# Seven products of quarters for eight in the last block's gate and value matmuls

## The chip, the cores and the metric

The kernel runs on one core of a Trainium2 chip. The metric is the device time of one execution in microseconds. The core's engines are TensorE (PE in the profile, its weight loads PEld), VectorE (DVE), ScalarE (ACT), GpSimd (POOL) and SyncE (SP), whose queue issues all DMA transfers of this kernel.

## The reference

Attention with a threshold (scores that lie more than tau below the row's maximum are dropped), followed by two gated layers; the first one normalises its input. Sizes: 4 batches, 8 heads, 576 positions, head size 64; so 2304 tokens of width 512, and an inner width of 1536. All data are float32.

```python
scores = scale * np.matmul(q, k.transpose(0, 1, 3, 2))
thresh = np.max(scores, axis=-1, keepdims=True) - tau
scores = np.where(scores >= thresh, scores, -1000000000.0)
scores = scores - np.max(scores, axis=-1, keepdims=True)
attn = np.exp(scores)
attn = attn / (np.sum(attn, axis=-1, keepdims=True) + 1e-09)
x = np.matmul(attn, v)                       # then tokens x (heads * 64)
xn = x / np.sqrt(np.mean(x * x, axis=-1, keepdims=True) + 1e-06) * rms_g
g = xn @ w_gate
x = (g * (1.0 / (1.0 + np.exp(-g)))) * (xn @ w_val) @ w_out
# second layer: the same with moe2_w_gate, moe2_w_val, moe2_w_out, without the norm
```

## The kernel before

The 2304 tokens are three blocks of 768 (`NB`, `TW`). A block's tokens lie along the columns: `X` holds its 4 chunks of 128 channels by 768 tokens. Attention of block 0 comes first and alone (`fast`); attention of block 1 and of block 2 (`tile_ops`, `pv`) is spread among the dense matmuls of the block before or two blocks before, so that the last block's dense matmuls run with no attention beside them.

The dense part (`moe`) has two layers of 18 units. Twelve units are gate-and-value units (`gate_val`), each for 128 of the 1536 inner channels; behind the fifth, the ninth and the twelfth of them come two units each of output products (`outp`). Every float32 operand is kept as a high and a low part in float32r, and a product is made of three matmuls (high by high, high by low, low by high). `dense` therefore issues, for one 128x768 result over 4 chunks of channels, 4 x 3 x 2 = 24 matmuls of 128x384, six to a piece; a gate-and-value unit has 48 of them. The results go by turns to two PSUM tiles of two banks each, `PB` and `PD` (`dense_ps`; in the profile all are `ps`, in the order of instructions ps1 and ps2). The gate's result goes through a tanh on ScalarE (L809) and a VectorE step (L810), the value's result through a second VectorE step (L821); `h`, the product, is split into its two parts by ScalarE (L825) and by VectorE or GpSimd (L828).

The weights of a unit are 128x1024 numbers. In block 0 they come from the inputs as 64-bit numbers and are converted (`weights`: three ScalarE steps, L737 to L739, and one on VectorE, L740), split into high and low part (`w_split`: ScalarE L702, VectorE or GpSimd L704) and stored to memory (`kept`). For the units in `K_E` only the whole number is stored and split again in blocks 1 and 2, for the others both parts are stored and loaded.

The order is made by a program at build time: each step has an engine, a cost in ns and a priority (`p=`), and a list scheduler (`Program.order`) goes through them, always taking on each engine the ready step with the smallest priority. The tables `NORM_E`, `HI_E`, `LO_E`, `V_E`, `W_E`, `H_E`, `X_E`, `P_E`, `EV_E` and `XO_E` choose the engine of steps that can run on more than one, and `UP`, `FP`, `T0`, `OFF`, `OFFF` and the like are the offsets of the priorities. Each engine then runs its queue strictly in that order.

Of the kernel before, what the change touches and what calls it, by code (L numbers as in the profile page):

```python
# [25 lines left out]
P = 128  # L26
# [9 lines left out]
NU = 18  # L36
# [47 lines left out]
NORM_E = [(0, 2, 0, 0, 2, 0, 0, 0, 1, 1, 0, 1), (1, 1, 1, 1, 0, 2, 1, 1, 2, 1, 1, 1), (1, 2, 2, 1, 0, 1, 1, 1, 0, 1, 2, 2)]  # L84
HI_E = [(2, 2, 2, 2, 2, 0, 1, 1, 1, 2, 2, 1), (2, 1, 0, 1, 0, 1, 0, 0, 1, 2, 2, 0), (0, 0, 0, 0, 0, 0, 1, 2, 2, 2, 0, 1)]
LO_E = [(0, 0, 2, 0, 2, 0, 0, 2, 2, 0, 0, 0), (0, 0, 2, 0, 2, 2, 0, 0, 0, 0, 0, 0), (0, 0, 2, 0, 2, 0, 0, 2, 0, 2, 0, 2)]


V_E = {0, 1, 4, 7, 8, 14, 15, 18, 20, 22, 25, 26, 27, 28, 29, 33, 35, 38, 41, 42, 44, 46, 47, 48, 50, 52, 57, 61}
# [12 lines left out]
EV_E = {0, 2, 5, 9, 12, 15, 20, 23, 27, 32, 33, 34, 37, 40, 43, 45, 46, 49, 51}
XO_E = {0, 2, 3, 4, 6, 8, 12, 17}
# [133 lines left out]
def body(ctx: ExitStack, tc: tile.TileContext, qkv, tau, w1, rg, w2, outT):  # L237
# [47 lines left out]
    r_raw = ring("raw", RAWN, [P, 2 * S], F32)  # L285
    r_v = ring("v", 3, [P, 5, 2, D], F32)
    r_v3 = ring("v3", 3, [P, 5, 64], BF16)
    ET = sb.tile([P, 4, S], F32, name="e")
# [22 lines left out]
    def SU(u):  # L311

        full = 36 * (NB - 1)
        if u <= full:
            return T0 + u * UP
        return T0 + full * UP + (u - full) * UL
# [649 lines left out]
```

## Time and profile before

| | |
|---|---|
| median of 3 runs | 1209.44 us (1208.04 to 1210.07) |
| profiled execution | 1210.33 us, of which the span of instructions 1208.5 us |
| mean granted TensorE clock | 0.997 |
| busy share of TensorE | 98% |
| busy shares of VectorE, ScalarE, GpSimd | 61%, 51%, 39% |
| last block behind its norm | from 898.8 to 1204.4 us of the span |

The profile gives each engine's busy time, tables of busy time by stretches, groups of instructions by line with their mean duration and the idle time before them, a list of who waited for whom, the chain of work that ended last, and the instructions in order of time. An end of a matmul is modelled, and matmuls overlap in the records: one lasts 0.34 us in them, while they start every 0.17 us.

### The profile page before, as it was taken

To read this page: it belongs to the slowest core of one execution; us is meant where nothing else is said; L and a number is where in the kernel's file an instruction comes from. 1 tells how busy PE (TensorE), PEld (TensorE's weight loads), DVE (VectorE), ACT (ScalarE), POOL (GpSimd) and SP (SyncE) were. 2 spreads that over 40 slices of the span, in tenths; PEclk is the share of its full clock that TensorE was granted. 3 is DMA by queue.
4 is the path that set the end of the run, shared out by engine and by line. 5 is a ranking of instruction groups with operands and counts; after the bars stand their busy time and mean duration, and the time that the engine had idled before them with its cause. 6 is when DMAs were issued, how large, how long until landed. Compare 5 with 4: busy or idle time off the path is not lost.

```text
span 1208.5 us, 18818 instructions
## 1 busy us (share of the span) xinstructions
PE 1178.9 (98%) x7252; PEld 1046.0 (87%) x7252; DVE 736.3 (61%) x1363; ACT 610.6 (51%) x827; POOL 468.2 (39%) x543
## 2 busy tenths in 40 slices
PE   7998889999999999999999999999999999999998
PEld 4565778888888888988888889888899999999998
DVE  7998686778868687576566576656543133332342
ACT  5779877878787877234434435434421222232211
POOL 1123256545666576434534636445320202220311
PEclk9999999999999999999999999999999999999999
DMA  7223758889689977665664554543344322212211
GB/s 231 87 87 130 277 147 267 264 224 266 185 232 244 252 236 191 149 198 155 177 146 112 125 146 110 124 128 75 92 135 145 105 88 70 93 65 87 71 53 53
DMA packets 173417, 181.98 MB, mean 151 GB/s; under 512 B 143760, under 2 KB 147344, under 8 KB 163344
## 3 DMA queue, kind: packets, MB, share of 16 engines
q1 hardware_dynamic: 173328, 180.78, 53.0%
q8 instruction: 57, 0.93, 0.3%
q14 instruction: 32, 0.26, 0.1%
HBM read 121.51 MB, written 30.93 MB: 126 GB/s over the span
## 4 chain that ended last, share of the span: by engine, by line
PE 90%; ACT 4%; DVE 4%; DMA 1%; issue 1%; SPq 0%; POOL 0%; ACTq 0%
PE ps L771 75%; PE ps L558 5%; PE pt L610 4%; PE pt L613 2%; PE pt L515 1%; PE ps L455 1%; ACT ag L541 1%; PE pt L494 1%; DMA w<-in_w 1%; DVE col L468 1%; ACT Y L399 1%; DVE Y L471 1%; ACT e L470 0%; DVE e L471 0%; ACT Y L470 0%
## 5 line engine op out<-in xcount | busy, mean ns | idle before, releaser
L771 PE MATMUL ps<-XS,w 128*128 128x384 f32 x3456 | 626.7, 340 | 5.7 <-DVE th L810 2.5
L771 PEld LDWEIGHTS ps<-XS,w 128*128 128x128 f32 x3456 | 598.8, 189 | 31.1 <-issue 21.4
L771 PE MATMUL ps<-h,w 128*128 128x384 f32 x1728 | 315.4, 339 | 0.0
L771 PEld LDWEIGHTS ps<-h,w 128*128 128x128 f32 x1728 | 300.5, 188 | 12.6 <-issue 11.0
L704 POOL TENSOR_TENSOR w<-w,w 128x1024 fp32r<-128x1024 f32 x37 | 90.0, 2433 | 141.9 <-ACT w L702 141.9
L810 DVE SCALAR_TENSOR_TENSOR th<-th,ps 128x768 f32<-128x768 f32 x70 | 66.7, 952 | 126.4 <-ACT th L809 126.2
L702 ACT CAST w<-w 128x1024 fp32r<-128x1024 f32 x80 | 84.0, 1049 | 107.2 <-PE ps L771 104.7
L809 ACT ACTIVATE th<-ps 128x768 f32<-128x768 f32 x70 | 56.8, 812 | 138.4 <-PE ps L771 138.4
L821 DVE SCALAR_TENSOR_TENSOR th<-th,ps 128x768 f32<-128x768 f32 x70 | 66.7, 952 | 86.4 <-PE ps L771 86.0
L575 DVE TENSOR_REDUCE col<-ps 128x1 f32<-128x576 f32 x96 | 72.4, 754 | 71.3 <-PE ps L558 71.2
L828 POOL TENSOR_TENSOR h<-th,h 128x768 fp32r<-128x768 f32 x30 | 57.3, 1909 | 134.9 <-ACT h L825 134.7
L577 ACT ACTIVATE e<-ps,col 128x576 f32<-128x576 f32 x96 | 70.8, 737 | 56.8 <-DVE col L576 53.1
L578 DVE SCALAR_TENSOR_TENSOR e<-ps,col,e 128x576 f32<-128x576 f32 x96 | 78.0, 813 | 35.2 <-ACT e L577 34.7
L825 ACT CAST h<-th 128x768 fp32r<-128x768 f32 x72 | 60.0, 834 | 75.7 <-DVE th L821 75.6
L418 POOL TENSOR_TENSOR e<-e,e 128x512 f16<-128x512 f32 x68 | 83.7, 1232 | 0.0
L857 DVE SCALAR_TENSOR_TENSOR Y<-ps,Y 128x768 f32<-128x768 f32 x48 | 45.9, 956 | 59.1 <-PE ps L771 58.9
L558 PE MATMUL ps<-raw 64*128 64x288 f32 (+1 forms) x416 | 72.2, 451 | 1.2 <-DVE e L578 1.2
L399 ACT ACTIVATE e<-e,col 128x576 f32<-128x576 f32 x60 | 51.8, 865 | 36.8 <-DVE col L588 27.3
L704 DVE TENSOR_TENSOR w<-w,w 128x1024 fp32r<-128x1024 f32 x43 | 58.9, 1369 | 13.8 <-ACT w L702 13.7
L828 DVE TENSOR_TENSOR h<-th,h 128x768 fp32r<-128x768 f32 x42 | 56.4, 1344 | 14.4 <-ACT h L825 14.3
L419 POOL TENSOR_TENSOR e<-e,e 128x64 f16<-128x64 f32 x68 | 28.8, 424 | 88.1 <-DVE e L412 38.7
L740 DVE SCALAR_TENSOR_TENSOR w<-w,t 128x1024 uint32<-128x1024 uint32 x36 | 49.7, 1381 | 10.4 <-ACT t L739 10.3
(110 smaller groups left out, 1263.2 us busy)
## 6 DMA issues: line engine op xcount, KB each, us to landing
w<-in_w SPq DMA_DIRECT2D x36, 1024.0 KB, 6.1
w<-kept SPq DMA_DIRECT2D x28, 1024.0 KB, 4.9
w<-kept SPq DMA_DIRECT2D x44, 512.0 KB, 3.8
kept<-w SPq DMA_DIRECT2D x14, 1024.0 KB, 6.1
kept<-w SPq DMA_DIRECT2D x22, 512.0 KB, 5.4
raw<-in_qkv SPq DMA_DIRECT2D x15, 576.0 KB, 4.4
v<-in_qkv SPq DMA_DIRECT2D x32, 160.0 KB, 3.1
raw<-in_qkv SPq DMA_DIRECT2D x16, 288.0 KB, 3.5
```

Of the source, the lines that this page charges most:

```text
L399: op("ACT", 760, lambda: nc.scalar.activation(e, e, AF.Identity, bias=c[:, 4:5], scale=c[:, 3:4]), **k)
L418: op(en, 601 if eng == 2 else 1128, lambda: n1.tensor_tensor(h[:, 640:], e[:, :512], h[:, :512], ALU.subtract), lock=True, w=[("lo", n)], ...
L558: nc.tensor.matmul(o[:, j], x[k, c0:c0 + w], x[k, S + j * HS:S + (j + 1) * HS], start=True, stop=True)
L575: op("DVE", 670, lambda: nc.vector.tensor_reduce(c[:, 0:1], s2, AX.XY, ALU.max, negate=True), w=[sk, ("mx", n)], bufs=[cb], p=T + F['MAX'] ...
L577: op("ACT", 640, lambda: nc.scalar.activation(e2, s2, AF.Exp, bias=c[:, 2:3], scale=SCALE), r=[("thr", n)], w=[sk, ("e", n)] + ek, bufs=[c ...
L578: op("DVE", 822, lambda: nc.vector.scalar_tensor_tensor(e2, s2, c[:, 1:2], e2, ALU.is_ge, ALU.mult, accum_out=c[:, 6:7]), r=[("thr", n)], ...
L702: op("ACT", 939, lambda: nc.scalar.copy(ws[:, 0], w), r=[("w32", n)], w=[("wh", n)], bufs=[b32, sbf], p=p, name=f"w_split{n}")
L704: op(en, 1142 if en == "DVE" else 2340, lambda: n1.tensor_tensor(ws[:, 1], w, f32(ws[:, 0]), ALU.subtract), lock=True, r=[("w32", n), ("wh ...
L771: nc.tensor.matmul(pt[:, j, :HT], w(i, a), x(i, b_)[:, j * HT:(j + 1) * HT], start=(i == 0 and a == 0 and b_ == 0), stop=(i == n - 1 and a ...
L810: op("DVE", 871, lambda: nc.vector.scalar_tensor_tensor(t2, t2, 1.0, g2, ALU.add, ALU.mult), lock=raw, w=gk + [("th", n)], bufs=[tb], p=T ...
L821: op("DVE", 871, lambda: nc.vector.scalar_tensor_tensor(t2, t2, 0.5, v2, ALU.mult, ALU.mult), lock=raw, w=vk + [("th", n)], bufs=[tb], p=T ...
L828: op(eng, 878 if eng == "DVE" else 1795, lambda: n1.tensor_tensor(h[:, 1], tb.t, f32(h[:, 0]), ALU.subtract), lock=True, r=[("th", n), ("h ...
```

## The change

In the last block, in each of the two layers, eleven of the twelve gate-and-value units (all but the first, `PLAIN = 1`) take a new path, `gate_val7`. Gate and value of a unit are seen as a product of two-by-two quarters: the columns are gate and value, the rows the two halves of the tokens (384 each), and the sum runs over the two halves of the channels. Seven products of quarters (Strassen's scheme in Winograd's form) take the place of eight. One product of quarters is 2 chunks x 3 = 6 matmuls of 128x384.

This needs sums of quarters of both operands. `combine` makes four sums of quarters of the block's `X` (in the second layer, of `Y`) on VectorE, casts their high parts on ScalarE and forms the low parts on GpSimd or VectorE (`T_E`). `weights7` loads a unit's whole weights, makes four sums of quarters (VectorE or GpSimd, `A_E`), so that 1024 columns become 1792, and splits all of them (ScalarE, then VectorE or GpSimd by `W_E`). Units outside `K_E` that take the new path need their whole weights as well, so 13 of them are stored a second time in block 0 (`kept2`). `K_E` itself has 17 units in place of 22.

The products accumulate in three banks of one 384-column result each, two sets of three by turns (`SETS`); the sums of products are gathered by ScalarE copies and VectorE additions into a buffer in `X` (`evac`), and some products accumulate onto what a bank holds already. The attention's buffers become slices of one tile, `arena`; when the attention is done, the same space holds the sums of quarters (`arena2`). Every priority offset and engine table has new values, and the scheduler's cost of a dense matmul is 173.4 ns in place of 162.7.

```diff
+ARENA = 17376
+PLAIN = 1
+GV = [m * NU + i for m in range(2) for i in [0, 1, 2, 3, 4, 7, 8, 9, 10, 13, 14, 15][PLAIN:]]
+A_E = {3, 5, 8, 9, 10, 12, 13, 14, 15, 16, 17, 18, 20, 21, 22, 24, 26, 28, 29, 31, 32, 33, 35}
+T_E = {0, 2, 3}
...
-EV_E = {0, 2, 5, 9, 12, 15, 20, 23, 27, 32, 33, 34, 37, 40, 43, 45, 46, 49, 51}
-XO_E = {0, 2, 3, 4, 6, 8, 12, 17}
+EV_E = {0, 35, 5, 37, 8, 9, 41, 12, 46, 15, 49, 19, 51, 23, 27}
+XO_E = {8, 17, 6}
...
+    r_s = Ring([lambda i=i: arena2()[:, 16 * HT + i * 3584:16 * HT + (i + 1) * 3584].rearrange("p (a c) -> p a c", a=2) for i in range(3)])
+    r_u = Ring([X.rearrange("p c s -> p (c s)")[:, i * 3 * HT:(i + 1) * 3 * HT].rearrange("p (u s) -> p u s", u=3) for i in range(2)])
...
+    def combine(x, keys, tmp, bufs, T, m):
+        B11, B12, B21, B22 = [x[:, i:i + 2, j * HT:(j + 1) * HT] for i in (0, 2) for j in (0, 1)]
...
+        steps = [(0, tmp, B12, B11, k0, []), (2, B12, B22, B12, k2, k0), (1, B22, B22, tmp, [], k2), (3, B21, B21, B22, [], k2)]
+        for i, (k, o, x0, x1, r, w) in enumerate(steps):
...
+            op("DVE", 920, lambda o=o, x0=x0, x1=x1: nc.vector.tensor_tensor(o, x0, x1, ALU.subtract), lock=True, r=r + d, w=w + [t], bufs=bufs, p=T + 1000 * i, name=f"comb{m}")
+            op("ACT", 734, lambda k=k, o=o: nc.scalar.copy(TS(0, k), o), r=w + [t], w=[("T0", m, k)], bufs=bufs + [b], p=T + 1000 * i + 200, name=f"comb{m}")
...
+            if n in kept2:
+                op("DMA", 1500, lambda: nc.sync.dma_start(kept2[n], w), r=[("w32", n)], w=[("kept", n)], bufs=[b32], p=T - 2000, name=f"keep{n}")
+
+    def weights7(n, i, T):
...
+        def sums():
+            n1.tensor_tensor(q(4), q(2), q(3), ALU.add)
+            n1.tensor_tensor(q(5), q(0), q(2), ALU.subtract)
+            n1.tensor_tensor(q(6), q(4), q(0), ALU.subtract)
+            n1.tensor_tensor(q(2), q(1), q(6), ALU.subtract)
...
+        op("ACT", 1690, lambda: nc.scalar.copy(sbf.t()[:, 0], st), r=[("w32", n)], w=[("wh", n)], bufs=[stb, sbf], p=p, name=f"w_split{n}")
...
+    SETS = [[(PA[:, 0, :HT], "PA0"), (PA[:, 1, :HT], "PA1"), (PC[:, :HT], "PC")], [(PE[:, :HT], "PE"), (PD[:, 0, :HT], "PD0"), (PD[:, 1, :HT], "PD1")]]
...
+                def product(pos, col, x, bank, key, first):
...
+                        for i in range(2):
+                            for a, b_ in ((0, 0), (0, 1), (1, 0)):
+                                nc.tensor.matmul(bank, w()[:, a, col * 256 + i * P:][:, :P], xf(i, b_), start=first and i == 0 and a == 0 and b_ == 0, stop=i == 1 and a == 1, skip_group_check=not first)
...
+                def evac(pos, i, bank, key, add):
...
+                    if add:
+                        op("DVE", 480, lambda: nc.vector.tensor_tensor(u3[:, i], u3[:, i], bank, ALU.add), **k)
+                    else:
+                        op("ACT", 390, lambda: nc.scalar.copy(u3[:, i], bank), **k)
+
+                product(-1, 4, ti(0), b2, k2, True)
+                evac(-1, 2, b2, k2, False)
+                product(1, 0, xi(0, 0), b1, k1, True)
+                evac(1, 0, b1, k1, False)
+                product(2, 1, xi(2, 0), b3, k3, True)
+                evac(2, 0, b3, k3, True)
+                product(3, 6, ti(1), b1, k1, False)
+                evac(3, 1, b1, k1, False)
+                product(4, 2, xi(2, 1), b2, k2, False)
+                evac(4, 1, b2, k2, True)
+                product(5, 5, ti(2), b1, k1, False)
+                evac(5, 2, b1, k1, True)
+                product(6.5, 3, ti(3), b1, k1, False)
```

The order of TensorE's instructions in the second layer of the last block, before: a unit fills one two-bank tile with 24 matmuls and then the other. `XS` is the operand, `w` the weights, ps1 and ps2 the tiles; the words in brackets name whom the instruction waits for.

```order
L771 MATMUL ps2_67<-XS_82,w2_120 128x384 [waits DMAHW7_49,DVE_49]
L771 MATMUL ps2_67<-XS_82,w2_120 128x384 x23
L771 MATMUL ps1_66<-XS_82,w2_120 128x384 [waits DVE_49]
L771 MATMUL ps1_66<-XS_82,w2_120 128x384 x23
L771 MATMUL ps2_67<-XS_82,w0_118 128x384 [waits DVE_49]
L771 MATMUL ps2_67<-XS_82,w0_118 128x384 x23
```

TensorE's order with the change, in the first layer of the last block behind the first output units. `arena2` holds the weights with their sums, and the sums of `X` too (then it is both operands); pt1 and the two halves of ps2 are one set of banks, the two halves of ps0 and pt0 the other.

```order
L891 MATMUL ps2_67<-XS_82,arena2_7416 128x384 [waits Activation_49]
L891 MATMUL ps2_67<-XS_82,arena2_7416 128x384 x5
L891 MATMUL pt1_69<-arena2_7416 128x384 [waits Activation_49]
L891 MATMUL pt1_69<-arena2_7416 128x384 x5
L891 MATMUL ps2_67<-XS_82,arena2_7416 128x384 [waits DVE_49]
L891 MATMUL ps2_67<-XS_82,arena2_7416 128x384 x5
L891 MATMUL pt1_69<-arena2_7416 128x384 [waits Activation_49]
L891 MATMUL pt1_69<-arena2_7416 128x384 x5
L891 MATMUL ps0_65<-arena2_7416 128x384 x2
L891 MATMUL ps0_65<-arena2_7416 128x384 [waits Pool_49]
L891 MATMUL ps0_65<-arena2_7416 128x384 x3
L891 MATMUL pt1_69<-arena2_7416 128x384 [waits DVE_49]
```

Where a wait stood before every 24th matmul, one now stands before nearly every sixth, for ScalarE's copies and VectorE's additions by turns; bank pt1 comes back after one other product.

ScalarE's order in the second layer of the last block, before: a tanh, a cast of `h` and at times a cast of weights (L702) per unit.

```order
L809 ACTIVATE th_111<-ps_67 128x768 [waits PE_49,Activation_49]
L825 CAST h_105<-th_111 128x768 [waits DVE_49]
L809 ACTIVATE th_110<-ps_67 128x768 [waits PE_49,Activation_49]
L702 CAST w_120<-w_115 128x1024 [waits DMAHW4_49,PE_49,Activation_49]
L825 CAST h_106<-th_110 128x768 [waits DVE_49]
L809 ACTIVATE th_111<-ps_67 128x768 [waits PE_49,Pool_49]
```

ScalarE's order with the change, in the first layer: L900 is the copy out of a bank, L917 the tanh, L971 the cast of `h`, L830 the cast of 1792 columns of weights.

```order
L917 ACTIVATE th_92<-X 128x768 [waits DVE_49]
L900 COPY X<-ps_65 128x384 [waits PE_49,Activation_49]
L830 CAST arena_7416<-w_94 128x1792 [waits DMAHW5_49,PE_49]
L900 COPY X<-ps_65 128x384 [waits PE_49]
L971 CAST h_90<-th_92 128x768 [waits DVE_49]
L900 COPY X<-ps_65 128x384 [waits PE_49,Pool_49]
L900 COPY X<-ps_67 128x384 [waits PE_49]
L917 ACTIVATE th_91<-X 128x768 [waits DVE_49]
L900 COPY X<-pt_69 128x384 [waits PE_49,Activation_49]
L830 CAST arena_7416<-w_93 128x1792 [waits DMAHW6_49,PE_49]
L900 COPY X<-pt_69 128x384 [waits PE_49]
```

Three copies per unit have come in, and a weight cast stands between two of them in every unit.

VectorE's order with the change, later in the first layer: L898 is the addition out of a bank, L918 to L921 the gate and value steps, L823 to L826 the four sums of weights, L832 the subtraction that makes the low parts of 1792 columns of weights.

```order
L898 TENSOR_TENSOR X<-X,ps_65 128x384 [waits PE_49,Activation_49]
L898 TENSOR_TENSOR X<-X,ps_65 128x384
L918 SCALAR_TENSOR_TENSOR th_91<-th_91,X 128x768 [waits Activation_49]
L823 TENSOR_TENSOR w_94<-w_94 128x256 [waits DMAHW7_49]
L824 TENSOR_TENSOR w_94<-w_94 128x256
L825 TENSOR_TENSOR w_94<-w_94 128x256 [waits DVE_49]
L826 TENSOR_TENSOR w_94<-w_94 128x256 [waits DVE_49]
L919 SCALAR_TENSOR_TENSOR th_91<-th_91,X 128x384
L898 TENSOR_TENSOR X<-X,ps_67 128x384 [waits PE_49,Activation_49]
L921 SCALAR_TENSOR_TENSOR th_91<-th_91,ps_65 128x384
L832 TENSOR_TENSOR arena_7416<-w_93,arena_7416 128x1792 [waits Activation_49]
L898 TENSOR_TENSOR X<-X,ps_67 128x384 [waits PE_49,Activation_49]
```

Before, this queue held two steps on the result, now and then an `h` subtraction (L828) and a weight subtraction (L704) per unit. Now additions that TensorE waits for stand among the sums and the subtraction of the weights.

## Rows read from the trace of the kernel before

**Rows 1.** The page: busy us, share of the span and instructions by engine.

```profile
PE 1178.9 (98%) x7252; PEld 1046.0 (87%) x7252; DVE 736.3 (61%) x1363; ACT 610.6 (51%) x827; POOL 468.2 (39%) x543
```

**Rows 2.** The chain that ended last, its end: start us, us, what.

```profile
898.77 305.60 PE ps L771 x1758
1204.39 0.96 DVE Y L857
```

**Rows 3.** By stage: busy us (instructions) by engine, clock, DMA share, GB/s.

```profile
0.00:120.00 120.00, 103.21 (x970) 66.86 (x970) 104.79 (x271) 88.92 (x170) 28.14 (x84) 1.00 0.42 132
...
0.00:180.00 180.00, 154.55 (x1274) 113.30 (x1275) 150.34 (x340) 137.42 (x230) 50.42 (x104) 0.98 0.50 159
180.00:480.00 300.00, 300.00 (x1697) 256.29 (x1697) 224.36 (x376) 237.12 (x279) 177.23 (x222) 1.00 0.86 237
480.00:900.00 420.00, 420.00 (x2534) 372.37 (x2533) 258.05 (x551) 160.53 (x235) 188.28 (x194) 1.00 0.54 135
900.00:1208.50 308.50, 304.36 (x1752) 303.99 (x1750) 103.56 (x98) 75.53 (x86) 52.29 (x25) 1.00 0.24 83
```

**Rows 4.** Who waited for whom: us in total, times, longest us.

```profile
PE ps L455 <- DMA raw<-in_qkv: 4.3, 2, 4.1
...
PE ps L771 <- POOL XS L693: 2.0, 1, 2.0
...
ACT w L737 <- DMA kept<-w: 4.8, 3, 2.2
```

**Rows 5.** Groups by line and form, 900 us to the end: busy, mean ns, idle before.

```profile
L704 POOL TENSOR_TENSOR w<-w,w 128x1024 fp32r<-128x1024 f32 x11 | 26.4, 2404 | 103.8 <-ACT w L702 103.8
L702 ACT CAST w<-w 128x1024 fp32r<-128x1024 f32 x22 | 23.1, 1052 | 77.6 <-PE ps L771 77.6
L810 DVE SCALAR_TENSOR_TENSOR th<-th,ps 128x768 f32<-128x768 f32 x24 | 22.9, 955 | 92.3 <-ACT th L809 92.3
...
L828 DVE TENSOR_TENSOR h<-th,h 128x768 fp32r<-128x768 f32 x14 | 20.7, 1477 | 9.0 <-ACT h L825 9.0
L825 ACT CAST h<-th 128x768 fp32r<-128x768 f32 x24 | 20.1, 836 | 41.5 <-DVE th L821 41.5
...
L857 DVE SCALAR_TENSOR_TENSOR Y<-ps,Y 128x768 f32<-128x768 f32 x18 | 17.2, 958 | 39.4 <-PE ps L771 39.3
L704 DVE TENSOR_TENSOR w<-w,w 128x1024 fp32r<-128x1024 f32 x11 | 13.4, 1218 | 6.2 <-ACT w L702 6.2
```

**Rows 6.** Groups by line and form, whole run: narrower steps on ScalarE and VectorE.

```profile
L541 ACT COPY ag<-pt 128x512 f32<-128x512 f32 x36 | 20.8, 599 | 6.7 <-PE pt L494 6.5
...
L539 DVE COPY ag<-pt 128x512 f32<-128x512 f32 x12 | 8.2, 684 | 1.0 <-PE pt L494 0.9
L541 ACT COPY ag<-pt 128x128 f32<-128x128 f32 x23 | 6.6, 288 | 2.3 <-PE pt L499 2.2
...
L628 DVE SCALAR_TENSOR_TENSOR X<-pt,pvt 64x384 f32<-64x384 f32 x8 | 4.4, 549 | 3.1 <-ACT pvt L623 3.1
...
L533 DVE TENSOR_TENSOR SS<-SS,sq 128x256 f32<-128x256 f32 x1 | 0.4, 418 | 0.0
```

**Rows 7.** In order of time, four places: start us, us, engine, line, instruction.

```profile
62.95 0.30 ACT L541 COPY ag<-pt 128x128 f32<-128x128 f32 x1
...
63.26 0.44 PE L494 MATMUL pt<-ident,e 128*128 128x128 f32 x2
...
1039.35 0.96 DVE L828 TENSOR_TENSOR h<-th,h 128x768 fp32r<-128x768 f32 x1 [0.90 <-ACT h L825]
...
1053.54 0.68 PE L771 MATMUL ps<-h,w 128*128 128x384 f32 x3
...
1054.26 0.96 DVE L857 SCALAR_TENSOR_TENSOR Y<-ps,Y 128x768 f32<-128x768 f32 x1 [1.37 <-PE ps L771]
...
1080.05 2.41 POOL L704 TENSOR_TENSOR w<-w,w 128x1024 fp32r<-128x1024 f32 x1 [4.11 <-ACT w L702]
...
1081.07 2.20 DVE L828 TENSOR_TENSOR h<-th,h 128x768 fp32r<-128x768 f32 x1 [0.90 <-ACT h L825]
```

More of the change, by code (lines that the diff above doesn't have):

```diff
@@ L82 @@
 NFG = NP * len(PHASES[0])
[L84 to L89, printed above, removed]
@@ L283, in body, with take @@
     SS = RB = sb.tile([P, TW], F32, name="SS")
[L285 to L288, printed above, removed]
+    AR = sb.tile([P, ARENA], F32, name="arena", tag="arena")
+    used = [0]
+    def take(n):
+        used[0] += n
+        assert used[0] <= ARENA
+        return AR[:, used[0] - n:used[0]]
+    r_raw = Ring([take(2 * S) for _ in range(RAWN)])
+    r_v = Ring([take(10 * D).rearrange("p (c a d) -> p c a d", c=5, a=2) for _ in range(3)])
+    r_v3 = Ring([take(160).bitcast(BF16).rearrange("p (c d) -> p c d", c=5) for _ in range(3)])
+    ET = take(4 * S).rearrange("p (i s) -> p i s", i=4)
     E4 = [ET[:, i] for i in range(4)]
@@ L292, in body @@
     r_ep = Ring([t for i in (0, 2) for t in (YE[:, i:i + 2], ET[:, i:i + 2])])
-    r_e16 = ring("e16", 3, [P, 2 * S], F16)
-    r_ag = ring("ag", 3, [P, 9, 384], F16)
-    TMP = [sb.tile([P, 384], F32, name=f"pvt{i}") for i in range(2)]
-    SQ = sb.tile([P, 384], F32, name="sq")
+    r_e16 = Ring([take(S).bitcast(F16) for _ in range(3)])
+    r_ag = Ring([take(9 * 192).bitcast(F16).rearrange("p (c q) -> p c q", c=9) for _ in range(3)])
+    TMP = [take(384) for _ in range(2)]
+    SQ = take(384)
     r_tmp = [Ring([t[h:h + 64] for t in TMP]) for h in (0, 64)]
@@ L315, in SU @@
             return T0 + u * UP
-        return T0 + full * UP + (u - full) * UL
+        return T0 + full * UP + sum(UL * (0.875 if i in GV else 1.0) for i in range(u - full))
     def ST(n):
@@ L698, in body @@
     w64, w32, wsp = {}, {}, {}
+    kept2 = {i: dr.tile([P, 1024], F32, name=f"kept2_{i}") for i in GV if i not in K_E}
     kept = [dr.tile([P, 2, 1024], F32, name=f"kept{i}") for i in range(2 * NU)]
@@ L708, in weights @@
         T = SU(n)
+        if n >= 2 * NU * (NB - 1) and n - 2 * NU * (NB - 1) in GV:
+            weights7(n, n - 2 * NU * (NB - 1), T)
+            return
         sbf = r_w.next()
@@ L864, in moe @@
             for f in range(NF):
+                if f == 0 and m == 1 and b == NB - 1:
+                    xb = Buf(None, xbuf)
+                    combine(Y, [[("Y", c)] for c in range(NC)], X[:, 3], [xb], SU(base), 1)
                 if f == 11 and m == 1:
```

135 lines of the change are left out of this document (106 added, 29 removed).

## Prediction

> **What bounds the kernel now.** Three views say where the time is, and in this order. The busy times of the whole run put TensorE at 98% [rows 1], but that is an average over four stages, so the second view is the table by stage [rows 3]. Up to 180 us TensorE is idle for 25 us and VectorE is the engine that is nearly full: in the first 120 us it works 104.8 us. From 180 us on TensorE is busy in every stretch, and the list of who waited for whom has no row for TensorE after 180 us; its largest, 4.3 us in total, lies before that point [rows 4]. The third view is the chain that ended last. Its last link but one is a single unbroken run of 1758 matmuls, 305.60 us [rows 2]. In the program 1758 is also the number of dense matmuls behind the last spread of the norm, so no record is missing and nothing stands between them: one matmul of 128x384 costs 305.60 / 1758 = 0.1738 us, the clock granted in full (1.00 in that stretch, the 2.4 GHz level) [rows 3]. A matmul taken out of this stretch takes 0.1738 us out of the span, as long as no other engine makes TensorE wait. The other engines have room: in the last 308 us VectorE works 103.6, ScalarE 75.5, GpSimd 52.3 us, and DMA is at a share of 0.24 [rows 3].
>
> **What is removed.** A gate-and-value unit has 48 matmuls before and 7 products of 6 = 42 after. Eleven of twelve units in each of two layers change, so 22 x 6 = 132 matmuls go; the order of instructions confirms it (5184 dense matmuls before, 5052 after, all the rest of TensorE's work equal in number). 132 x 0.1738 = **22.9 us off**, all on the path.
>
> **What is added on the path: a bank that must be emptied in time.** Before, an output tile was filled by 24 matmuls, and the next 24 went to the other tile, so its readers had some 4 us. Now a product has 6 matmuls, and its bank is used again after one other product. There are three such close re-uses in a unit (the fourth, sixth and seventh product on bank b1), 66 in all; 44 wait for a copy by ScalarE, 22 for an addition by VectorE. From the start of a product's last matmul to the first matmul that needs the bank are 7 matmuls = 1.22 us. Needed in this time: the reader starts 0.38 us after the last matmul's start (the third matmul of the row at 1053.54 starts two periods later, at 1053.88, VectorE at 1054.26); ScalarE's copy of 384 columns takes 0.50 us (0.288 for 128 and 0.599 for 512 columns, on the line between); VectorE's 384-column step from PSUM takes 0.55; TensorE goes on about 0.01 after ScalarE's end (62.95 + 0.30, then 63.26) [rows 6, 7]. That leaves 0.33 us of slack behind ScalarE and 0.28 behind VectorE. If the engine is free the re-use costs nothing, so the lower bound is 0; a gain is excluded, since TensorE has no idle time there to give back.
>
> The engines are not always free. By the rows of the last stretch a weight cast of 1792 columns costs 1.052 x 1.75 = 1.84 us on ScalarE, the subtraction 1.218 x 1.75 = 2.13 us on VectorE or 2.404 x 1.75 = 4.21 us on GpSimd (estimates in proportion to the columns) [rows 5]. The tables of the change put 15 of 22 subtractions and 15 of 22 sets of four weight sums on VectorE. ScalarE then has 75.5 us from before, less 14 of its 22 casts of 1024 (14.7), plus 22 casts (40.5), 66 copies (32.7) and 8 casts of operands (6.7): 141 of some 286 us. VectorE has 103.6 + 66 additions (36) + 60 sums at 0.418 (25) + 15 subtractions (32) + about 5 others: some 200 of 286 us [rows 3, 5, 6]. If the close re-uses met their engine at a random moment, the mean wait for one is the sum over the engine's instructions of (duration - slack)^2 / 2, divided by 286 us. ScalarE: 22 casts give 25.1, some 72 instructions of 0.84 give 9.2; 34.3 / 286 = 0.12 us, times 44 = 5.3 us. VectorE: 15 subtractions 25.7, 50 instructions of 0.955 11.5, 11 h subtractions of 1.48 7.9, the short ones 4.6; 49.7 / 286 = 0.17 us, times 22 = 3.8 us. Random arrival would cost 9.1 us. The order shows the evacuations standing among the long instructions, not behind several of them, so I take the middle between 0 and 9.1: **5 us**.
>
> **What is added beside the path.** The sums of quarters of X wait for the norm and stand beside the output products of block 1 and the plain first unit (48 matmuls, 8.3 us), which is there as cover: 4 VectorE subtractions of 0.96, a cast of 0.84 each and 3 GpSimd subtractions of 2.4 x 0.75 = 1.8 us form a queue of about 7 us that starts before the plain unit. In the second layer they also wait for the last sums of Y. A wait for operands of this kind took 2.0 us before, at the first norm, and none was left at the later ones [rows 4]. Bounds 0 and 2 us; I take 0.5, since the first products want only the sums that come first.
>
> **DMA in the first block.** 13 extra stores of 0.5 MB, and 5 units more that keep both parts (another 0.5 MB each), are 18 x 0.524 = 9.4 MB more to write between 180 and 480 us. There the engines moved 237 GB/s at a share of 0.86, so 275 GB/s when full: 34 us of the 300, where 42 are free [rows 3]. Cost 0 while it fits; without that cover it is the third rival. A store of this kind also holds one of two buffers for 1024 columns; ScalarE waited 4.8 us for that before [rows 4], TensorE not at all.
>
> **The new order of the first 900 us.** All priorities and engine choices are new. From 180 us on TensorE is full, with the same instructions, so a new order can only lose there; I put 0. Before 180 us it can go either way. VectorE, the fullest engine, gives 3 copies of 512 columns (0.684) and 5 short ones (some 0.28, as ScalarE's 0.288) to ScalarE, 3.5 us in all [rows 6]. I bound the effect by plus and minus 3.5 us and take a gain of 1, nearer to nothing, as many chains there alternate between the engines.
>
> **Sum.** -22.9 + 5 + 0.5 - 1 = -18.4 us against the profiled execution of 1210.33 us (span 1208.5 and 1.8 around it): 1191.9. That execution stands 0.9 above the median of the runs, 1209.44, so the prediction for the median is **1191 us**. Its own range: all gains and no wait, -22.9 - 3.5, is 1183; all costs, -22.9 + 9.1 + 2 + 3.5, is 1201.
>
> **A rule that speaks against it.** One row shows VectorE's h subtraction taking 2.20 us from 1081.07, while GpSimd ran its weight subtraction from 1080.05 for 2.41 us; alone it took 0.96 at 1039.35 [rows 7]. VectorE's end, 1083.27, is 0.81 after GpSimd's: it did next to nothing before. The Trainium skill, SBUF — State Buffer, section "SBUF: two separate sides", says that the two engines share a pair of ports by an exclusive lock held for the whole instruction, and the trace agrees with that here. By that rule, a VectorE instruction with two operands from SBUF, and every addition queued behind it, waits for GpSimd.
>
> **The rivals.**
> 1. *Port lock.* The mechanism of that row at the 7 weight subtractions on GpSimd, 4.21 us each: if each catches a subtraction on VectorE with a close addition queued behind it, half of it is left on the mean, 2 us, 7 x 2 = 14 us more: 1205. For it: VectorE is at 70%. Against: only 22 of the re-uses wait for VectorE.
> 2. *Weights ahead of evacuations* (the slower side). If in each unit the cast of 1.84 us on ScalarE stands just ahead of a close copy, TensorE loses 1.84 - 0.33 = 1.5 us per unit, 33 us in all, in place of the 5: 1209.4 - 22.9 + 0.5 - 1 + 33 = 1219. It decides from 23.4 / 22 = 1.06 us per unit on. For it: ScalarE's queue has a cast between two copies in most units. Against: the cast can start as soon as a copy has been done and has a whole period of 1.0 us and more before the next close one.
> 3. *DMA of the first block.* If the 34 us don't find the free 42, since all transfers stand in one queue, and half of it comes out as waits for weights: 17 us more, 1208.
> 4. *More than forecast.* No waits and more than 3.5 us won at the start: below 1183.
>
> That the seven products aren't what runs can be left out: the count of matmuls shows it.
>
> **How the numbers follow.** Forecast 0.66, port lock 0.14, weights ahead 0.08, DMA 0.05, more 0.07. The range takes in the forecast and the first rival, 1183 to 1205, which is 0.8. About 0.2% (2.4 us) is what a measurement of this kernel can tell from no change: under 1207.0 lie the forecast, the port lock and the fourth, 0.87; within it the third, 0.05; above it the second, 0.08.
>
> **What would show it.** In the profile after: TensorE's busy stretch behind the last norm shorter by some 18 us; rows of TensorE waiting for the copies (ScalarE) and additions (VectorE) of the new units, some 5 us in all, none over 1.5; the mean time of a matmul unchanged at 0.174; no waits for weights between 180 and 480 us with DMA's share near 0.95; the first dense stretch beginning within 3.5 us of before. Wrong would be: waits of 1 us in every unit (second rival), VectorE's subtractions of the weights at 4 us and more (first), or a first block that has become longer (third).

## The result, and the profile after

| | before | after |
|---|---|---|
| median of 4 runs | 1208.88 us (1208.04 to 1210.07) | 1197.30 us (1195.39 to 1197.88) |
| ratio | | 0.990, 95% interval 0.988 to 0.992 |
| span of the profiled execution | 1208.5 us | 1193.6 us |

The kernel became 11.6 us faster, 1%; 18.4 were forecast. The profiled execution of after is the fastest of its four runs, 1.9 us below their median, and that of before stands 1.4 above its own, so a comparison of the two traces shows 15.0 us (the start of the last VectorE step, 1204.39 in [rows 2] and 1189.38 below).

The first view is the page's list of engines, to be read beside [rows 1]:

```profile
PE 1158.8 (97%) x7120; PEld 1017.9 (85%) x7120; DVE 839.7 (70%) x1518; ACT 663.5 (56%) x911; POOL 514.7 (43%) x575
```

7252 - 7120 = 132 matmuls went, as counted. The table by stage answers to [rows 3] (busy us and instructions of PE, PEld, DVE, ACT, POOL, then clock, DMA share, GB/s):

```profile
0.00:180.00 180.00, 159.73 (x1329) 118.43 (x1330) 148.96 (x341) 141.23 (x240) 41.15 (x101) 1.00 0.50 162
180.00:480.00 300.00, 298.32 (x1691) 253.87 (x1689) 230.62 (x381) 236.21 (x277) 182.29 (x226) 1.00 0.91 260
480.00:900.00 420.00, 418.82 (x2525) 371.91 (x2524) 269.30 (x557) 167.22 (x239) 204.00 (x208) 1.00 0.57 153
900.00:1193.60 293.60, 281.90 (x1581) 273.68 (x1579) 190.82 (x242) 118.85 (x155) 87.29 (x41) 1.00 0.18 63
```

TensorE idles 20.3 us up to 180 us (before 25.4), 2.9 between 180 and 900 (before 0), and in the last block behind 900 us 11.7, of which 4.2 lie behind its end: 7.5 us that weren't there before. What it waits for in the last block is best read from the rows of the weight loads (who waited for whom, PEld from 880 us on: us in total, times, longest us); in the last stretch before, this list was empty:

```profile
PEld ps L891 <- DVE X L898: 6.8, 11, 1.9
PEld ps L891 <- ACT X L900: 6.7, 12, 0.9
PEld ps L891 <- DVE th L921: 0.8, 1, 0.8
PEld ps L859 <- DVE h L974: 0.7, 1, 0.7
PEld ps L859 <- DVE Y L1003: 0.3, 1, 0.3
```

26 waits, 15.3 us. What TensorE lost in all follows from the chain that ended last, which enters the first product of the new kind at 888.95 (start us, us, what):

```profile
888.95 1.04 PE pt L891 x6
...
1173.63 15.73 PE ps L859 x90
1189.36 0.02 issue
1189.38 0.96 DVE Y L1003
```

From there to the end of the last matmul, 1189.36, lie 1644 matmuls of 128x384, which take 285.8 us at 0.1738 each. They took 300.4, so **14.6 us** were lost; before, 1758 of them stood without a gap [rows 2]. The forecast had 5. The 7.5 us of idle time above are less, as the modelled ends of the matmuls cover a part of every wait. This loss of the 1644 matmuls is given below for the other kernels too, from their traces.

The place where the largest of the regular waits arises, in order of time (start us, us, engine, line; in brackets how long the engine had been idle and for whom). L891 is a product, L900 a copy out of a bank:

```profile
1003.68 1.31 PE L891 MATMUL ps<-arena 128*128 128x384 f32 x6
...
1004.83 1.21 PE L891 MATMUL ps<-XS,arena 128*128 128x384 f32 x6
1006.07 0.48 ACT L900 COPY X<-ps 128x384 f32<-128x384 f32 x1 [2.44 <-PE ps L891]
1006.60 2.04 PEld L891 LDWEIGHTS ps<-arena 128*128 128x128 f32 x12 [0.89 <-ACT X L900]
1006.60 3.63 PE L891 MATMUL ps<-arena 128*128 128x384 f32 x17 [0.57 <-ACT X L900]
1008.02 1.02 DVE L898 TENSOR_TENSOR X<-X,ps 128x384 f32<-128x384 f32 x2 [3.59 <-PE ps L891]
...
1009.09 1.00 PEld L891 LDWEIGHTS ps<-arena 128*128 128x128 f32 x6 [0.46 <-DVE X L898]
```

The product of 1003.68 is the fourth of the unit, in bank PA0, and ends at 1004.99. Its copy starts at 1006.07, though ScalarE has been idle for 2.44 us. What ends at 1006.04 is the next product, in PA1, the other half of the same tile. TensorE's next product wants PA0 and waits 0.89 us. The two additions of 1008.02 show the same from the other side: the first of them reads PA1, whose product ended at 1006.04, yet both start only when a later product in PA0 has ended. So a reader of one half waits for what was last written into the other half as well. It is the program that makes it wait: dependencies are kept for a two-bank PSUM tile as one thing, and the semaphore waits in the built program say so. Of the 154 reads of banks in the new units (66 copies, 66 additions, 22 last steps), 29 wait for a product in the neighbouring half that was issued after their own, 24 of them for the very next product; among the reads of PC and PE, tiles of one bank, there is none.

Sorted by what the late releaser itself had waited for, the 26 waits are: 15 for the neighbouring half (8.4 us in the loads' rows), 4 for ScalarE behind a weight cast (1.6), 5 for a VectorE that was busy (4.3), and 2 in the output units (1.0).

### The profile page after: what moved, and what is told of

The parts are those of the page before. It is cut to its first block, busy times and chain, and to the rows that moved or that the text cites. A ratio compares the mean times of both kernels' runs of the same rounds, so it can differ in the third digit from the quotient of the medians.

```text
span 1193.6 us, 18854 instructions
## 1 busy us (share of the span) xinstructions
PE 1158.8 (97%) x7120; PEld 1017.9 (85%) x7120; DVE 839.7 (70%) x1518; ACT 663.5 (56%) x911; POOL 514.7 (43%) x575
## 4 chain that ended last, share of the span: by engine, by line
PE 81%; DVE 8%; ACT 5%; DMA 3%; issue 2%; POOL 1%; SPq 0%; DVEq 0%; ACTq 0%; POOLq 0%
PE ps L859 55%; PE ps L891 8%; PE ps L596 5%; PE pt L648 4%; PE pt L891 4%; PE pt L651 2%; PE pt L553 1%; PE ps L493 1%; DMA arena<-arena 1%; DMA arena<-in_qkv 1%; DVE X L898 1%; PE pt L532 1%; ACT arena L579 1%; DVE col L506 1%; DVE Y L509 1%
## 5 line engine op out<-in xcount | busy, mean ns | idle before, releaser
L859 PE MATMUL ps<-XS,w 128*128 128x384 f32 x2400 | 442.3, 340 | 5.1 <-DVE th L953 3.0
L859 PEld LDWEIGHTS ps<-XS,w 128*128 128x128 f32 x2400 | 412.3, 188 | 33.8 <-issue 25.8
L616 DVE SCALAR_TENSOR_TENSOR arena<-ps,col,arena 128x576 f32<-128x576 f32 x96 | 78.2, 815 | 43.0 <-ACT arena L615 41.5
L615 ACT ACTIVATE arena<-ps,col 128x576 f32<-128x576 f32 x96 | 70.8, 738 | 65.7 <-DVE col L614 59.2
L762 ACT CAST w<-w 128x1024 fp32r<-128x1024 f32 x61 | 64.0, 1049 | 50.6 <-PE ps L859 42.8
L971 ACT CAST h<-th 128x768 fp32r<-128x768 f32 x72 | 60.0, 833 | 41.1 <-DVE th L964 27.1
L891 PE MATMUL ps<-arena 128*128 128x384 f32 x348 | 70.6, 340 | 5.5 <-ACT X L900 2.6
L596 PE MATMUL ps<-arena 64*128 64x288 f32 (+1 forms) x416 | 72.2, 451 | 1.2 <-DVE arena L616 1.2
L456 POOL TENSOR_TENSOR arena<-arena 128x512 f16<-128x512 f32 x60 | 72.9, 1215 | 0.0
L891 PEld LDWEIGHTS ps<-arena 128*128 128x128 f32 x348 | 60.1, 188 | 10.6 <-DVE X L898 4.9
L964 DVE SCALAR_TENSOR_TENSOR th<-th,ps 128x768 f32<-128x768 f32 x48 | 45.7, 952 | 31.8 <-PE ps L859 31.4
L953 DVE SCALAR_TENSOR_TENSOR th<-th,ps 128x768 f32<-128x768 f32 x48 | 45.6, 949 | 31.5 <-ACT th L952 31.3
L437 ACT ACTIVATE arena<-arena,col 128x576 f32<-128x576 f32 x60 | 51.6, 864 | 22.2 <-DVE col L626 20.4
```

The costliest lines, as they stand in the source:

```text
L437: op("ACT", 760, lambda: nc.scalar.activation(e, e, AF.Identity, bias=c[:, 4:5], scale=c[:, 3:4]), **k)
L456: op(en, 601 if eng == 2 else 1128, lambda: n1.tensor_tensor(h[:, 640:], e[:, :512], h[:, :512], ALU.subtract), lock=True, w=[("lo", n)], ...
L596: nc.tensor.matmul(o[:, j], x[k, c0:c0 + w], x[k, S + j * HS:S + (j + 1) * HS], start=True, stop=True)
L615: op("ACT", 640, lambda: nc.scalar.activation(e2, s2, AF.Exp, bias=c[:, 2:3], scale=SCALE), r=[("thr", n)], w=[*sk, ("e", n)] + ek, bufs=[ ...
L616: op("DVE", 822, lambda: nc.vector.scalar_tensor_tensor(e2, s2, c[:, 1:2], e2, ALU.is_ge, ALU.mult, accum_out=c[:, 6:7]), r=[("thr", n)], ...
L762: op("ACT", 939, lambda: nc.scalar.copy(ws[:, 0], w), r=[("w32", n)], w=[("wh", n)], bufs=[b32, sbf], p=p, name=f"w_split{n}")
```

## The experiments

Theory A: the waits come from tiles of two banks. Theory B: the evacuations are late because their engines are busy, the port lock between VectorE and GpSimd among it. Theory C: one product between two uses of a bank is too short in any case. Ratios stand against the kernel before on the same chip; the changed kernel has 0.990 [0.988, 0.992]. The texts put on record number the experiments otherwise than they stand here: their first is the one with another bank, their second the one with no neighbours, their fourth the one without GpSimd, their sixth the one without the weight casts.

**Another bank for the product that comes back most.**

```diff
-    SETS = [[(PA[:, 0, :HT], "PA0"), (PA[:, 1, :HT], "PA1"), (PC[:, :HT], "PC")], [(PE[:, :HT], "PE"), (PD[:, 0, :HT], "PD0"), (PD[:, 1, :HT], "PD1")]]
+    SETS = [[(PC[:, :HT], "PC"), (PA[:, 0, :HT], "PA0"), (PA[:, 1, :HT], "PA1")], [(PE[:, :HT], "PE"), (PD[:, 0, :HT], "PD0"), (PD[:, 1, :HT], "PD1")]]
```

> One line differs from the changed kernel: in the first set of banks the bank that is re-used most (b1) is the single-bank tile PC, and the other two products of the set take the halves of PA; the order of all instructions stays as it was. Theory A (a reader of one half of a two-bank tile waits for the product in its other half, and the next product there for that reader): of the 15.3 us of TensorE's waits in the last block, 6.1 us are such waits on PA; they go, TensorE's waits in the last block fall to 9 or 10 us, and the kernel to 1190 to 1192.5 us. Theory B (the evacuations come late because VectorE and ScalarE are busy, GpSimd's port lock among it): nothing changes, 1196 to 1198.5 us. Theory C (one product between two uses of a bank is too short even with idle engines): nothing changes either, since the distances stay the same.

Measured: 1188.86 us, ratio 0.983 [0.981, 0.984]; 8.4 us less than the changed kernel, with every instruction in its old place, and 1.1 below Theory A's range. The last block's waits (loads' rows) are these:

```profile
PEld ps L891 <- ACT X L900: 1.3, 2, 0.9
PEld ps L891 <- DVE X L898: 1.1, 2, 0.6
PEld ps L859 <- DVE h L974: 0.7, 1, 0.7
PEld pt L891 <- ACT X L900: 0.6, 1, 0.6
PEld ps L859 <- DVE Y L1003: 0.3, 1, 0.3
```

7 waits with 4.0 us; the 1644 matmuls lose 4.3 us in place of 14.6. The same unit as before, in order of time:

```profile
1004.42 1.21 PE L891 MATMUL pt<-arena 128*128 128x384 f32 x6
...
1005.46 1.21 PE L891 MATMUL ps<-XS,arena 128*128 128x384 f32 x6
1005.66 0.48 ACT L900 COPY X<-pt 128x384 f32<-128x384 f32 x1 [1.55 <-PE pt L891]
1006.51 1.20 PE L891 MATMUL pt<-arena 128*128 128x384 f32 x6
```

The fourth product ends at 1005.63, its copy starts at 1005.66 while the fifth product runs, and the sixth starts without a gap. Theory A holds. Theories B and C fall as main causes: engines and distances are as they were. More went than the waits I had put down to the halves: of the 9 for busy engines 6 went too. As nothing else was changed, they hung on the same coupling; that a queue was pushed back by a reader at its head that waited is the likely way, not one that a run singles out.

**The same banks, but two tiles.** `LA(0)` and `LA(1)` take the place of PA's halves; at their first use PA's pool is closed, and its two banks become two tiles.

```diff
-    PA, PB, PD = [ps.tile([P, 2, 512], F32, name=f"ps{i}") for i in range(3)]
+    PB, PD = [ps.tile([P, 2, 512], F32, name=f"ps{i}") for i in (1, 2)]
+    PA = psa.enter_context(tc.tile_pool(name="psa", bufs=1, space=bass.MemoryType.PSUM)).tile([P, 2, 512], F32, name="ps0")
...
+    def LA(j):
+        if not late_a:
+            psa.close()
+            pool = psa.enter_context(tc.tile_pool(name="psb", bufs=1, space=bass.MemoryType.PSUM))
+            late_a.extend(pool.tile([P, 512], F32, name=f"pa{i}") for i in range(2))
```

> The changed kernel with its own banks and its own order of instructions; only PA, which is one tile of two banks, becomes two tiles of one bank each after the last norm. Unlike the first experiment no product changes its bank's place in the set. Theory A (waits go by tiles of two banks, not by banks): as there, 7 to 9 us less than the changed kernel, 1188 to 1190.5 us. If it was the choice of the bank itself that helped there (PC free earlier than PA, or another distance), nothing happens here: 1196 to 1198.5 us.

Measured: 1188.68 us, ratio 0.983 [0.981, 0.984], 7 waits with 4.1 us, a loss of 4.1. It isn't the choice of the bank, it is the tile.

**No neighbours in a unit at all.** The tiles of the last experiment, with other sets:

```diff
-    SETS = [[(PA[:, 0, :HT], "PA0"), (PA[:, 1, :HT], "PA1"), (PC[:, :HT], "PC")], [(PE[:, :HT], "PE"), (PD[:, 0, :HT], "PD0"), (PD[:, 1, :HT], "PD1")]]
+    SETS = [[(lambda: PC[:, :HT], "PC"), (lambda: LA(0), "PA0"), (lambda: PD[:, 0, :HT], "PD0")], [(lambda: PE[:, :HT], "PE"), (lambda: LA(1), "PA1"), (lambda: PD[:, 1, :HT], "PD1")]]
```

> Theory A's full remedy: PA becomes two tiles of one bank each once the attention and the last norm are done, and the sets are PC, half of PA, half of PD and PE, other half of PA, other half of PD, so that no product and its reader have a neighbour in the same tile within a unit; the scheduler sees other banks and may order the last block a little differently. Theory A: 8.4 us of waits go (all that are not explained by a busy VectorE or ScalarE), TensorE's waits in the last block fall to 7 us, 1188 to 1190.5 us. Theories B and C: 1196 to 1198.5 us.

Measured: **1186.86 us, ratio 0.981 [0.980, 0.983]**, the lowest time of all (the times alone don't tell it from the two before), 1.1 below Theory A's range. What is left of the last block's waits:

```profile
PEld ps L870 <- DVE h L985: 0.7, 1, 0.7
PEld pt L902 <- ACT X L911: 0.5, 1, 0.5
PEld ps L870 <- DVE Y L1014: 0.3, 1, 0.3
```

One wait of a new unit, 0.5 us; the loss is 1.6. With 22 casts, 66 copies and 15 subtractions in the queues, busy engines cost next to nothing once the readers may start. The reads that wait for a neighbour number 29, 10, 7 and 0 in the changed kernel and these three experiments (in the order after, swapped, split, none), the losses of the 1644 matmuls are 14.6, 4.3, 4.1 and 1.6 us, and the times 1197.3, 1188.9, 1188.7 and 1186.9.

**The new tables without the seven products.**

```diff
-GV = [m * NU + i for m in range(2) for i in [0, 1, 2, 3, 4, 7, 8, 9, 10, 13, 14, 15][PLAIN:]]
+GV_STORED = [m * NU + i for m in range(2) for i in [0, 1, 2, 3, 4, 7, 8, 9, 10, 13, 14, 15][PLAIN:]]
+GV = []
...
-    kept2 = {i: dr.tile([P, 1024], F32, name=f"kept2_{i}") for i in GV if i not in K_E}
+    kept2 = {i: dr.tile([P, 1024], F32, name=f"kept2_{i}") for i in GV_STORED if i not in K_E}
```

> All of the change's tables, buffers and extra stores, but the last block's units take the old path with eight products (5184 dense matmuls again, no sums of quarters). Reading of the two traces: at 900 us the changed kernel was 39 dense matmuls ahead, 6.8 us, won in the first 180 us by the new order, and the seven products are worth 22.9 - 15.3 = 7.6 us less some tenths. Then this kernel has no waits of TensorE in the last block and takes 1202 to 1205 us. Rival: the lead at 900 us is no gain of the front but work put off, and the seven products alone make the difference: 1208 to 1210 us.

Measured: 1207.30 us, ratio 0.998 [0.997, 1.000]. It lies between the two expectations, nearer to the rival. The count behind the first was right for the two traces: at 900 us only 128x384 matmuls are left in either kernel, and after had 39 fewer of them to do than the 132 account for. But it is one execution, and without the new units the scheduler orders everything anew from about 440 us on, so that this kernel's front isn't the changed kernel's. The new tables and the extra stores together are worth 2 us here, and the seven products of the changed kernel 10 (1207.3 against 1197.3), where the loss in the last block leaves 22.9 - 14.6 = 8.3; the rest lies ahead of that block. The last block has two waits of 0.3 and 0.2 us here.

**Without GpSimd in the last block.** Three lines like this one:

```diff
-        op(en, 2200 if en == "DVE" else 4200, lambda: n2.tensor_tensor(sbf.t()[:, 1], st, f32(sbf.t()[:, 0]), ALU.subtract), lock=True,
+        op(en, 2200 if en == "DVE" else 4200, lambda z=(16 if en == "POOL" and i not in GV[:3] else 1792): n2.tensor_tensor(sbf.t()[:, 1, :z], st[:, :z], f32(sbf.t()[:, 0, :z]), ALU.subtract), lock=True,
```

> The changed kernel with GpSimd's subtractions of the last block cut to 16 columns: the low parts of h, and of the weights from the fourth unit on, are left out there (the sums of weights on GpSimd and the sums of X and Y are whole). The order stays. Theory A: only the waits behind a VectorE that GpSimd holds up go, the largest of which is 1.9 us at 1131 us of the span, 2 to 3.5 us in all: 1193.5 to 1195.5 us. Theory B with the port lock as the cause: VectorE loses some 30 us of its time to GpSimd in the last block, and with it most of the 6.8 us that TensorE waits for VectorE's additions goes: 1189 to 1191 us.

Measured: 1196.54 us, ratio 0.990 [0.988, 0.991]: no difference from the changed kernel that can be told. The last stretch:

```profile
900.00:1192.80 292.80, 283.05 (x1591) 275.16 (x1589) 166.40 (x243) 119.57 (x156) 34.55 (x41) 1.00 0.18 63
```

VectorE works 166.4 us in place of 190.8 with the same instructions of its own, so GpSimd takes 24.4 us from it in the changed kernel; it has the time to spare. Neither expectation is met. In the trace the 1644 matmuls lose 12.2 us in place of 14.6, which is the 2 to 3.5 us less that Theory A had, though the median shows 0.8 only; the port lock isn't what makes up most of the loss.

**Without the weight casts.** The same cut on ScalarE (L830 and L762).

> The changed kernel with ScalarE's casts of weights in the last block cut to 16 columns (the high parts are left out there, from the fourth unit of seven products on); the order stays. Theory A: only four of the waits for ScalarE (at 916.4, 955.1, 963.7 and 1081.4 us) stand behind a cast, 1.6 us in the weight loads' rows and 0.9 in matmul starts: 1195.5 to 1197.5 us. The second rival of the prediction (weights ahead of evacuations): the 12 waits for ScalarE's copies go, 1190 to 1193 us.

Measured: 1214.75 us, ratio 1.003 [1.002, 1.004]. Less work, and 17 us slower than the changed kernel; no theory had this. The profiled execution is the fastest of the twelve, 1208.97 us; in it the loads' waits in the last block are 25.3 us, 13.6 of them for VectorE's additions and 4.3 for one step of L921. Where the 4.3 arise, in order of time:

```profile
1124.05 0.55 DVE L898 TENSOR_TENSOR X<-X,ps 128x384 f32<-128x384 f32 x1
1124.17 4.00 POOL L832 TENSOR_TENSOR arena<-w,arena 128x1792 fp32r<-128x1792 f32 x1 [21.83 <-DVE th L919]
1124.52 3.94 DVE L823 TENSOR_TENSOR w<-w 128x256 f32<-128x256 f32 x1
...
1128.38 0.41 DVE L824 TENSOR_TENSOR w<-w 128x256 f32<-128x256 f32 x1
1128.71 0.41 DVE L825 TENSOR_TENSOR w<-w 128x256 f32<-128x256 f32 x1
1129.16 0.43 DVE L826 TENSOR_TENSOR w<-w 128x256 f32<-128x256 f32 x1
1129.50 0.55 DVE L921 SCALAR_TENSOR_TENSOR th<-th,ps 128x384 f32<-128x384 f32 x1
...
1130.10 0.45 PE L891 MATMUL ps<-arena 128*128 128x384 f32 x1 [3.98 <-DVE th L921]
```

A VectorE sum of 0.41 us takes 3.94, until GpSimd's subtraction ends at 1128.17; behind it L921 has to empty the bank that TensorE wants. In the changed kernel the same GpSimd instruction comes a few steps later in VectorE's queue, because ScalarE's cast of 1.70 us stands ahead of it:

```profile
1117.11 1.70 ACT L830 CAST arena<-w 128x1792 fp32r<-128x1792 f32 x1 [1.32 <-PE ps L891]
...
1117.72 0.42 DVE L823 TENSOR_TENSOR w<-w 128x256 f32<-128x256 f32 x1
...
1118.84 0.43 DVE L826 TENSOR_TENSOR w<-w 128x256 f32<-128x256 f32 x1
1118.88 4.31 POOL L832 TENSOR_TENSOR arena<-w,arena 128x1792 fp32r<-128x1792 f32 x1 [22.49 <-DVE w L825]
1119.19 0.55 DVE L921 SCALAR_TENSOR_TENSOR th<-th,ps 128x384 f32<-128x384 f32 x1
1119.65 0.55 DVE L898 TENSOR_TENSOR X<-X,ps 128x384 f32<-128x384 f32 x1
...
1121.38 2.63 DVE L918 SCALAR_TENSOR_TENSOR th<-th,X 128x768 f32<-128x768 f32 x1 [1.18 <-ACT th L917]
```

The four sums are over when GpSimd starts, L921 and the addition run beside it at their usual 0.55 us, and only L918 is held (2.63), which TensorE doesn't wait for. The same happens to a VectorE sum at 924.12 (4.10 us) and at 939.07 (3.96), with waits of TensorE of 3.7 and 2.7 us behind them.

Waits aren't all of it. Behind the two longest of them, at 929.22 and 1130.10, the granted clock fell to half, the 1.2 GHz level (columns as in the table by stage):

```profile
929.82:933.23 3.41, 3.41 (x13) 3.40 (x12) 1.66 (x3) 1.51 (x2) 0.00 (x0) 0.50 0.20 78
...
1131.21:1134.62 3.41, 3.41 (x13) 3.41 (x12) 2.41 (x2) 0.82 (x2) 1.61 (x1) 0.50 0.00 0
```

TensorE was busy throughout, so half of these 6.8 us, 3.4, is lost. The 1644 matmuls lose 27.7 us in this trace, 13.1 more than in the changed kernel, whose clock stays full up to its last matmul. The other eleven executions show a mean clock of 0.991 to 0.994 (this one 0.995, the changed kernel 0.997 to 1.000) and left no trace, so how the 17 us of the medians divide between waits and clock is open.

**Both cuts together**, to tell whether that is the cause:

> The sixth and the fourth experiment together: in the last block the casts of weights on ScalarE and GpSimd's subtractions are cut to 16 columns (high and low parts left out as there). The sixth alone was 17 us slower than the changed kernel. Theory L: without the cast GpSimd's subtraction of the weights starts 1.5 us earlier and then runs beside VectorE's sums of weights, which stand still until it ends (3.9 us in place of 0.42 at 1124.5 us), with the additions TensorE waits for behind them; with GpSimd's work gone too, the slowdown goes: 1194 to 1197.5 us. Theory D: the early end of the cast moves VectorE's or ScalarE's own queue, whatever GpSimd does: 1208 to 1215 us.

Measured: 1195.82 us, ratio 0.989 [0.986, 0.991]. Without GpSimd's subtractions the slowdown is gone, and the clock stays full in the last block (the loss is 11.4 us). The port lock is what starts it.

**Without the second stores** (on the best version; `kept2[n]` becomes `kept2[n][:, :16]`, and the last block loads `kept[i][:, 0]`):

> The kernel of the second experiment, in its order, with the 13 second stores of whole weights cut to 16 columns (the last block loads the high part in their place, so its result is another). Between 180 and 900 us TensorE idles some 4 us there, in the kernel before nothing; 1.3 us of it are waits for a DMA. Theory: the extra stores cost what that wait shows, 0 to 1.5 us: 1185.3 to 1187.5 us. The third rival of the prediction (DMA of the first block): all of the idle time there comes from transfers that stand behind the stores, 3 to 4.5 us: 1182.4 to 1184 us.

Measured: 1187.97 us, ratio 0.982 [0.981, 0.983], against 0.981 [0.980, 0.983] with them, 0.5 us above the first range. The stores cost nothing that can be measured. The idle time between 180 and 900 us stays (4.5 us, 3.8 with the stores), so they aren't its cause.

**Without the plain unit** (on the best version, `PLAIN = 0`):

> The kernel of the second experiment with no plain unit at the start of the layers: all twelve units of each layer take seven products. 12 matmuls less are 2.1 us. If the sums of quarters come in time behind the last outputs of the block before, it takes 1184.5 to 1186 us. If the plain unit is the cover that the prediction took it for, TensorE waits up to 7 us in each layer for the sums' queue: 1189 to 1199 us. The scheduler orders other things anew as well, so differences under 2 us in the stretch before 880 us say nothing here.

Measured: 1188.18 us, ratio 0.983 [0.982, 0.984], between the two expectations. 12 matmuls less, 2.1 us, bring nothing: the loss goes from 1.6 to 4.3 us. The last block's waits in the loads' rows are 4.5 us in 6 in place of 1.5 in 3, and the last VectorE step starts at 1181.68 in place of 1180.35. So the cover is worth what it costs, but the wait of 7 us per layer that would be there without it isn't seen.

## Why the prediction was right, and where it was not

The time lies in the range, the sign is right, and the gain is 0.63 of the forecast. By the prediction's own steps, in the two traces:

1. *132 matmuls, 22.9 us.* Right: the count agrees, and a dense run of 156 matmuls in the trace after lasts 27.10 us, 0.1737 each.
2. *A bank that must be emptied in time, 5 us.* Wrong in the mechanism, and 9.6 us short. The failed step is "its bank is used again after one other product" with "7 matmuls = 1.22 us" behind it: that time runs only if the reader may start when its own product is done. Where the product in between lies in the other half of the tile, the reader starts behind that, and the re-use waits for all of 0.38 + 0.48 us, 0.89 in the loads' rows. Measured were 14.6 us, above the bound for random arrival (9.1), which was thought to be the worst; the longest wait was 1.9 us where none over 1.5 was to be seen, and the busy stretch behind the norm became 8 us shorter, not 18. And what the 5 us were made of, queues on ScalarE and VectorE, costs at most 1.6 us when the tiles are apart (the experiment with no neighbours). The trace of before couldn't show the coupling, as both halves of a tile were always filled and read as one there; but the order of the change names `ps2` for two of a set's three banks, and the question to put was whether dependencies go by that name.
3. *Sums of quarters, 0.5 us.* No wait for them is in the list of after.
4. *DMA in the first block, 0.* Right as a price (the run without the stores), with a share of 0.91 where 0.95 was said.
5. *New order, -1 within 3.5.* Outside the bound in the two traces. The matmuls behind the last norm start at 898.8 us before and at 888.95 + 18 x 0.1738 = 892.1 after, 6.7 us earlier. 2.3 of it are idle time (5.2 us less up to 180 us, 2.9 more up to 900). Up to 3.4 are the clock: before, it stood at half for 3.41 us from 133.80 and again from 164.52, with TensorE busy for nearly all of both (behind waits of 1.8 and 2.5 us), and after nowhere until the end. The last 1 us is open. This is one execution of each: in the seven other kernels here with the same order up to the last block that point lies between 892.4 and 897.8 us, so after's trace is the earliest of eight. In the medians some 3 us are left for the front (11.6 - 8.3), and the run without the seven products, whose order is another, gives about 2. "From 180 us on a new order can only lose" held for idle time, but it wasn't 0; what makes the 2.9 us is open.

The sum in the trace: -22.9 + 14.6 - 6.7 = -15.0. That the total fell into the range is in part luck: the bank term came out far above its bound, and the front gave some of it back. Without that gain the time would have been some 1209.4 - 22.9 + 14.6 = 1201 us, at the end of the forecast's own range (1201).

The first rival's mechanism is in the trace and costs VectorE 24.4 us, but TensorE only 2.4. It was right to give it little weight and wrong to reckon its price as half a subtraction for each of the seven on GpSimd (14 us): it is a matter of which VectorE instruction stands beside GpSimd's, and a start earlier by some 1.5 us turned it into 17 us, the clock's part included. The second rival (casts ahead of copies) is refuted: without the casts the waits for ScalarE went from 6.7 to 5.1 us only. The third is refuted by the run without stores.

A rule that had seemed to be met: the Trainium skill, Perfetto Trace Analysis, section "Optimizing Tensor Performance", says that independent groups of matmuls should rotate through different PSUM banks so that the evacuation of one overlaps the matmuls of the next. The change did that, bank by bank, and still lost 14.6 us, and 1.6 once no unit had two banks of one tile: banks of one tile didn't count as different.

## What to carry to other kernels

Where products rotate through banks, give each bank a tile of its own, or put the bank that comes back soonest into one; then check in the trace that the reader starts when *its* product ends, not the next. A wait that comes back with the same length (0.89 us five times here, 0.46 to 0.49 seven times) hints at a dependency; behind busy engines the waits had all lengths from 0.2 to 1.9 us. Count what is lost by the matmuls themselves, so many at their usual distance against the time they took, and look at the granted clock behind every long wait. And an experiment that takes work away can be slower: before concluding that the work was useful, look at what it starts earlier, and beside whom.

## What the runs showed of the hardware that was not expected

GpSimd holds VectorE up only for some instructions. VectorE steps with both operands in SBUF stood still until GpSimd's subtraction ended (L823 3.94 us in place of 0.41, L918 2.63 in place of 0.95); additions and products with one operand in PSUM ran beside the same subtraction at their usual 0.55 us (1119.19 and 1119.65). The Trainium skill, SBUF — State Buffer, section "SBUF: two separate sides", has it so: beside a GpSimd instruction that reads SBUF, the lock concerns those of VectorE's instructions that have two inputs from SBUF (and some fast modes). The trace agrees, and it is why the evacuations survived beside GpSimd; they are hurt only when such a two-input step stands ahead of them in the queue.

A wait of TensorE can cost more than its length. Without the weight casts the granted clock fell to half for 3.41 us just behind the waits of 3.7 and 4.3 us (in the loads' rows), and six matmuls took 2.12 us at 930.83 and at 1131.29 in place of 1.20; behind the shorter waits of that block it stayed full. The runs give no rule for it: before, it fell behind a wait of 2.5 us (at 164.52), and after, it stayed full behind one of 3.0 us (at 155.35).
